# Row sums of the last two heads by ones in 32-column tiles, a 256-column part in the model's second layer, and a plan with every place moved

## The chip, the cores and the metric

The kernel runs on one core of one Trainium2 chip. The metric is device time in microseconds (us); the kernel before took 472.49 us, the median of three runs (470.97 to 474.16). Five engines share the work, each with its own queue in program order: TensorE (PE, with its weight loads shown apart as PEld), VectorE (DVE), ScalarE (ACT), GpSimd (POOL) and SyncE (SP), which here issues nearly all DMAs. Matmul results go to PSUM, from where DVE or ACT fetch them; a buffer in PSUM or SBUF can be written again only when its last reader is done.

## The reference

Two stages follow one another. The first is attention over 4 batches of 8 heads, 768 positions, 64 wide, in which a query sees only keys of its own hash bucket (six sign bits of a projection). The second is a soft mixture of experts on the attention's output.

```python
q_bits = (np.einsum('bhsd,dk->bhsk', q, proj) > 0); k_bits = (np.einsum('bhsd,dk->bhsk', k, proj) > 0)
mask = q_bucket[:, :, :, None] == k_bucket[:, :, None, :]
scores = np.where(mask, scale * np.matmul(q, k.transpose(0, 1, 3, 2)), -1e9)
attn = np.exp(scores - np.max(scores, axis=-1, keepdims=True))
out = np.matmul(attn / (np.sum(attn, axis=-1, keepdims=True) + 1e-09), v)
...
logits = x @ phi                       # x: 3072 rows of 512, phi: 512 x 32
d = softmax of logits over the rows;  slot_input = d.T @ x
h = np.maximum(slot_input[e] @ w1[e], 0.0);  slot_out[e] = h @ w2[e]     # 8 experts, 512 -> 1024 -> 512
c = softmax of logits over the slots; return c @ slot_out
```

## The kernel before

**Heads.** The 32 heads run one after another, overlapped by a plan. A head's 768 x 768 table is made six row tiles of 128 at a time. `smax` (L692) multiplies a tile's Y rows without exponent to find each row's maximum, which `most` (L701, L704) takes on DVE from one of two PSUM buffers (`p_sm`); `shift` (L730 to L733) turns a head's maxima into shifts on DVE, `shift_rows` (L740, L743) transposes them on PE, copies them on ACT and sends them into row 64 of X by a DMA. `scores` (L755) then makes the table again, in three PSUM buffers (`p_st`), and `exps` (L761) takes the exponential on ACT. `acc` (L769, L772) adds the six tiles up on POOL, for the last head's last three tiles on DVE; `av` (L782) multiplies them by v in tiles of 32 columns of the array, four at a time. A table tile is 768 columns, made as 512 and 256, so half of the `smax` and `scores` matmuls are 512 columns wide and half 256.

**Row sums.** For two heads together `pair_sum` (L794) multiplies `acc` by ones in 32-column tiles, ACT copies the result, `pair_turn` (L801, L803) transposes it on DVE and takes the reciprocal, `pair_rec` (L807, L811) transposes back. The last two heads, 30 and 31, go singly: `one_tok` (L852) loads six 128 x 128 blocks of `acc` as weights and multiplies them by one column of ones, `one_r` (L856, L857) adds eps and takes reciprocals, `one_rec` (L864) spreads them by 12 matmuls with the identity into PSUM, and `one_mul` (L869) multiplies the head's output by them. `one_log` (L879) and `one_fold` (L875) make the last batch's logits, `one_x` (L883) turns the output for the slots; then `batch_max`, `batch_exp`, `batch_turn` (L948) and `batch_slots` (L961) follow. After every batch of eight heads the same work runs in the plan as `batch_both` to `batch_arrange`. `spin_in` and `batch_spin` (L1034) turn stored weights of earlier batches.

**The plan.** No engine's order is written out line by line. Every call above gets a place, a number in slots (six slots to a head): WHEN holds the places of a typical even and odd head, FIRST those of the first heads, LAST those of the last two, counted from the end. The calls are sorted by place (L1132) and issued in that order, and each call puts its instructions, DMAs included, at the end of the queues of its engines. So a place sets the order on every engine's queue, and nothing else.

**Prologue.** `bits`, `split_hi`, `split_lo`, `first_x`, `bits_rest` prepare heads 0 and 1 on ACT, DVE and POOL; `shift_first(0)` and `rows_first(0)` (L711 to L713, L720 to L722) shift the first four row tiles of head 0, `shift_first(1)` and `rows_first(1)` the last two. `keep_busy` fills PE with idle matmuls.

**Weights.** Pieces of 512 KB of w1 and w2 are loaded by SP: 21 in the plan, one in six slots (`load_weights`), 24 more as the attention's pools are freed from slot `last - 14` on (L1134 to L1165), the rest while the model runs.

**Model.** `hidden` (L1202), `turned` (L1216), then `model` (L1255) makes four parts of 128 output columns:

```python
    PART = tuple((n // 2, n % 2 * P, P) for n in range(KC))
    for i in range(KC):
        model(i, 1)
        so = split_out(i)
        if i < KC - 1:
            begin(i + 1)
            model(i + 1, 0, range(5))
        send(so, i)
```

`split_out` (L1263, L1264) copies a part in two halves of precision, `send` (L1278, L1281) multiplies it by the slot weights in six pieces and issues the output's DMAs on SP, for the last part six of 256 KB (L1283).

Of the kernel before, what the change touches and what calls it, by code (L numbers as in the profile page):

```python
# [76 lines left out]

FIRST = {('bits', 0): -72.6747,
 ('first_x', 0): -27.9008,
 ('first_x', 1): -26.1415,  # L80
 ('first_x', 2): -26.8579,
 ('first_x', 3): -23.1972,
 ('load', 4, 0): -6.8513,
 ('load', 4, 1): -8.037,
 ('bits', 2): -24.4068,
 ('split_hi', 2): -8.1664,
 ('split_lo', 2, 0): -2.6064,
 ('split_lo', 2, 1): -1.9761,
 ('spread_y', 2): -5.503,
 ('spread_bits', 2): -10.0455,  # L90
 ('spread_l', 2): 0.6012,
 ('spread_x', 2): 9.7073,
 ('smax', 1, 0, 0): -18.3027,
 ('smax', 1, 0, 1): -7.7987,
 ('smax', 1, 1, 0): -7.7809,
 ('smax', 1, 1, 1): -16.5074,
 ('smax', 1, 2, 0): -1.6546,
 ('smax', 1, 2, 1): -7.0969,
 ('smax', 1, 3, 0): -5.3473,
 ('smax', 1, 3, 1): -10.2117,  # L100
 ('smax', 1, 4, 0): -2.2645,
 ('smax', 1, 4, 1): -10.1613,
 ('smax', 1, 5, 0): -8.0819,
 ('smax', 1, 5, 1): -8.3095,
 ('first_y', 1): -42.2836,
 ('first_y', 2): -15.549,
 ('spread_y', 1): -27.7984,
 ('spread_l', 0): -14.408,
 ('spread_bits', 1): -27.0534,
 ('bits_rest',): -34.7942,  # L110
 ('bits_copy', 0): -63.6382,
 ('bits_copy', 1): -58.3416,
 ('first_w', 0, 0): -62.1853,
 ('first_w', 0, 1): -41.4124,
 ('copy_ident',): -20.1322,
 ('bits_out',): -18.4901,
# [4 lines left out]
 ('most', 1, 0): -16.7983,
 ('most', 1, 2): -2.8602,
 ('most', 1, 3): -12.717,
 ('most', 1, 4): -0.0617,
 ('most', 1, 6): -0.8205,
 ('most', 1, 7): -8.2722,
 ('most', 1, 8): -0.5381,
 ('most', 1, 10): -4.2243,
# [1 line left out]
 ('bits_first', 1): -42.1244,  # L130
 ('split_hi', 0): -71.0276,
 ('split_lo', 0, 0): -34.7937,
 ('split_lo', 0, 1): -31.3679,
 ('spread_x', 0): -8.3415,
 ('load_v', 0): -32.8507,
 ('smax', 0, 0, 0): -43.5236,
# [1 line left out]
 ('most', 0, 0): -31.9163,
 ('exps', 0, 0): -11.5103,
 ('smax', 0, 0, 1): -39.8038,  # L140
 ('scores', 0, 0, 1): -11.555,
 ('smax', 0, 1, 0): -37.4567,
 ('scores', 0, 1, 0): -10.1798,
 ('most', 0, 2): -23.5156,
 ('exps', 0, 2): -6.5408,
 ('smax', 0, 1, 1): -63.9296,
 ('scores', 0, 1, 1): -4.3102,
 ('most', 0, 3): -32.8132,
 ('exps', 0, 3): -1.9067,
 ('smax', 0, 2, 0): -40.7538,  # L150
 ('scores', 0, 2, 0): -10.1532,
 ('most', 0, 4): -24.1099,
 ('exps', 0, 4): -6.3229,
 ('smax', 0, 2, 1): -31.6426,
 ('scores', 0, 2, 1): -5.5744,
 ('smax', 0, 3, 0): -30.4598,
 ('scores', 0, 3, 0): -2.022,
 ('most', 0, 6): -22.6441,
 ('exps', 0, 6): -0.8279,
 ('smax', 0, 3, 1): -41.857,  # L160
 ('scores', 0, 3, 1): -1.0568,
 ('most', 0, 7): -31.2096,
 ('exps', 0, 7): 0.3214,
 ('smax', 0, 4, 0): -19.3974,
 ('scores', 0, 4, 0): -13.0479,
 ('most', 0, 8): -18.0237,
 ('exps', 0, 8): -8.3163,
 ('smax', 0, 4, 1): -25.1431,
 ('scores', 0, 4, 1): -8.0065,
 ('smax', 0, 5, 0): -25.0975,  # L170
 ('scores', 0, 5, 0): -3.2765,
 ('most', 0, 10): -20.1124,
 ('exps', 0, 10): 0.0515,
 ('smax', 0, 5, 1): -29.6765,
 ('scores', 0, 5, 1): 0.6417,
 ('most', 0, 11): -20.2405,
 ('exps', 0, 11): 7.3801,
 ('av', 0, 0): -6.448,
 ('acc', 0, 1): 1.236,
 ('av', 0, 1): 0.222,  # L180
 ('acc', 0, 2): 3.5659,
 ('av', 0, 2): 2.2158,
 ('acc', 0, 3): 11.2521,
 ('av', 0, 3): 2.5799,
 ('acc', 0, 4): 12.2768,
 ('av', 0, 4): 7.1934,
 ('acc', 0, 5): 17.6795,
 ('av', 0, 5): 10.6193,
 ('spread_l', 1): -19.2874,
 ('spread_x', 1): -11.4653,  # L190
 ('load_v', 1): -62.3718,
 ('scores', 1, 0, 0): 5.8215,
 ('exps', 1, 0): 7.9587,
 ('scores', 1, 0, 1): 3.0669,
 ('scores', 1, 1, 0): 5.1281,
 ('exps', 1, 2): 7.8346,
 ('scores', 1, 1, 1): 3.5907,
 ('exps', 1, 3): 5.8224,
 ('scores', 1, 2, 0): 6.602,
 ('exps', 1, 4): 8.2456,  # L200
 ('scores', 1, 2, 1): 7.8818,
 ('scores', 1, 3, 0): 8.0524,
 ('exps', 1, 6): 8.2514,
 ('scores', 1, 3, 1): 7.1217,
 ('exps', 1, 7): 9.5937,
 ('scores', 1, 4, 0): 11.0381,
 ('exps', 1, 8): 11.4237,
 ('scores', 1, 4, 1): 9.5798,
 ('scores', 1, 5, 0): 11.0927,
 ('exps', 1, 10): 11.6836,  # L210
 ('scores', 1, 5, 1): 11.3223,
 ('exps', 1, 11): 14.6309,
 ('shift', 1): 0.3343,
 ('shift_rows', 1): 1.0244,
 ('av', 1, 0): 11.4569,
 ('acc', 1, 1): 9.0913,
 ('av', 1, 1): 12.1564,
 ('acc', 1, 2): 9.4434,
 ('av', 1, 2): 12.4636,
 ('acc', 1, 3): 16.034,  # L220
 ('av', 1, 3): 13.6761,
 ('acc', 1, 4): 18.0104,
 ('av', 1, 4): 15.8205,
 ('acc', 1, 5): 18.0227,
 ('av', 1, 5): 17.6592,
 ('load', 2, 0): -41.9391,
 ('load', 2, 1): -33.0335,
 ('load_v', 2): 15.3736,
 ('smax', 2, 0, 0): -0.969,
 ('scores', 2, 0, 0): 11.9422,  # L230
 ('most', 2, 0): 1.6034,
 ('exps', 2, 0): 12.8561,
 ('smax', 2, 0, 1): 2.6468,
 ('scores', 2, 0, 1): 19.2511,
 ('smax', 2, 1, 0): 2.7151,
 ('scores', 2, 1, 0): 20.0695,
 ('most', 2, 2): 5.8071,
 ('exps', 2, 2): 20.2977,
 ('smax', 2, 1, 1): 4.3747,
 ('scores', 2, 1, 1): 18.8979,  # L240
 ('most', 2, 3): 6.6984,
 ('exps', 2, 3): 19.3969,
 ('smax', 2, 2, 0): 5.8812,
 ('scores', 2, 2, 0): 14.0957,
 ('most', 2, 4): 9.3359,
 ('exps', 2, 4): 17.0111,
 ('smax', 2, 2, 1): 1.5133,
 ('scores', 2, 2, 1): 17.6289,
 ('smax', 2, 3, 0): 1.9085,
 ('scores', 2, 3, 0): 20.2039,  # L250
 ('most', 2, 6): 4.1541,
 ('exps', 2, 6): 20.5254,
 ('smax', 2, 3, 1): 2.3419,
 ('scores', 2, 3, 1): 18.51,
 ('most', 2, 7): 4.1671,
 ('exps', 2, 7): 18.6459,
 ('smax', 2, 4, 0): 0.3426,
 ('scores', 2, 4, 0): 20.2573,
 ('most', 2, 8): 3.8721,
 ('exps', 2, 8): 20.5597,  # L260
 ('smax', 2, 4, 1): 5.5737,
 ('scores', 2, 4, 1): 13.7623,
 ('smax', 2, 5, 0): 5.8534,
 ('scores', 2, 5, 0): 14.5864,
 ('most', 2, 10): 9.2668,
 ('exps', 2, 10): 17.0626,
 ('smax', 2, 5, 1): 2.5531,
 ('scores', 2, 5, 1): 11.9948,
 ('most', 2, 11): 5.9084,
# [1071 lines left out]
```

## Time and profile before

| | |
|---|---|
| runs | 470.97, 472.49, 474.16 us (median 472.49) |
| the profiled execution | 473.32 us, span 471.5 us |
| PE busy | 452.6 us, 96% |
| POOL, DVE, ACT busy | 342.2, 358.1, 277.2 us (73%, 76%, 59%) |
| mean granted clock of PE | 0.989 |

The span runs from the first to the last instruction; the profiled execution's own time is 1.8 us longer. A row of a timeline gives start, duration, engine, line, operation, `out<-in`, shapes and how many instructions are merged; the bracket at its end gives the idle time of that engine just before it and what ended it. Matmul rows overlap their successors, so the cost of a group of matmuls is read from start to start.

### The profile page before, as it was taken

How to read it: one execution, taken by the hardware profiler on the slowest of the kernel's cores; microseconds unless marked ns; L12 is line 12 of the kernel's file. 1: busy time of each engine (PE TensorE's matmuls, PEld its weight loads, DVE VectorE, ACT ScalarE, POOL GpSimd, SP SyncE). 2: the span in 40 equal slices, each digit the busy share in tenths (PEclk: the TensorE clock that was granted, in tenths of full speed). 3: DMA queues.
4: the chain of work that ended last, by engine and by line, in shares of the span. 5: the costliest groups of instructions: out<-in, count | busy, mean ns of one | idle time of the engine just before them, and what ended most of it. 6: DMA issues, size and time to landing. Idle time of an engine off the chain costs nothing.

```text
span 471.5 us, 11017 instructions
## 1 busy us (share of the span) xinstructions
PE 452.6 (96%) x4159; PEld 284.8 (60%) x4159; DVE 358.1 (76%) x680; ACT 277.2 (59%) x569; POOL 342.2 (73%) x209
## 2 busy tenths in 40 slices
PE   8899999999999999999999999999999999979993
PEld 6555757575756566666665566666565755553782
DVE  5766879898989897978798989898989864454241
...
GB/s 207 173 74 177 151 188 184 191 181 180 193 187 182 130 198 159 214 154 219 157 215 159 208 130 236 138 148 129 149 136 90 100 202 384 307 358 332 411 310 265
DMA packets 37704, 93.21 MB, mean 198 GB/s; under 512 B 7106, under 2 KB 13380, under 8 KB 37652
## 3 DMA queue, kind: packets, MB, share of 16 engines
...
## 4 chain that ended last, share of the span: by engine, by line
PE 78%; DVE 9%; DMA 7%; issue 2%; SPq 1%; ACT 1%; DVEq 0%; POOL 0%; ACTq 0%
PE st L755 25%; PE av L782 20%; PE smx L692 14%; DVE w L596 3%; PE qs L1255 3%; PE qh L1202 3%; DVE mx L704 3%; DMA v<-vt 2%; PE mi L794 2%; PE mi L639 2%; PE mi L819 2%; DMA w<-w 1%; SPq L600 1%; PE mi L740 1%; DMA fold<-cst 1%
## 5 line engine op out<-in xcount | busy, mean ns | idle before, releaser
L772 POOL TENSOR_TENSOR acc<-acc,pt 128x768 f32<-128x768 f32 x125 | 246.4, 1977 | 7.6 <-ACT pt L761 1.0
L761 ACT ACTIVATE pt<-st 128x512 f32<-128x512 f32 x288 | 160.3, 595 | 55.8 <-PE st L755 52.6
L755 PE MATMUL st<-XY 128*128 128x256 f32 (+1 forms) x768 | 175.0, 343 | 0.4 <-DMA XY<-mr 0.2
L704 DVE TENSOR_REDUCE mx<-smx 128x1 f32<-128x512 f32 x192 | 130.6, 688 | 20.3 <-PE smx L692 17.0
L755 PEld LDWEIGHTS st<-XY 128*128 128x128 f32 x768 | 127.3, 190 | 23.1 <-ACT pt L761 4.3
L782 PE MATMUL av<-pt,v 128*32 128x384 f32 x1536 | 136.0, 489 | 0.5 <-DMA v<-vt 0.5
L692 PE MATMUL smx<-XY 96*128 96x512 f32 (+1 forms) x384 | 116.0, 361 | 4.5 <-DVE mx L704 2.5
L692 PEld LDWEIGHTS smx<-XY 96*128 96x128 f32 x384 | 67.9, 190 | 36.4 <-DVE mx L704 15.8
L782 PEld LDWEIGHTS av<-pt,v 128*32 128x32 f32 x1536 | 46.8, 110 | 69.8 <-issue 66.4
L769 POOL TENSOR_TENSOR acc<-pt 128x768 f32<-128x768 f32 x32 | 61.1, 1908 | 32.1 <-ACT pt L761 31.9
L701 DVE TENSOR_REDUCE mx<-smx 128x2 f32<-128x512 f32 x96 | 65.7, 685 | 9.2 <-PE smx L692 8.5
L596 DVE TENSOR_TENSOR w<-raw,w 128x768 fp32r<-128x768 f32 x28 | 39.4, 1407 | 6.2 <-ACT w L592 5.6
L786 ACT COPY avs<-av 128x384 f32<-128x384 f32 x32 | 15.4, 480 | 28.3 <-PE av L782 28.3
L797 ACT ACTIVATE sm<-mi,eps 128x384 f32<-128x384 f32 x15 | 8.7, 582 | 27.1 <-PE mi L794 27.0
L592 ACT CAST w<-raw 128x768 fp32r<-128x768 f32 x30 | 23.6, 832 | 0.8 <-DMA XY<-mr 0.5
L609 ACT CAST XY<-w 64x768 fp32r<-64x768 f32 x30 | 23.4, 830 | 0.0
L811 ACT COPY r<-rt 64x12 f32<-64x12 f32 x60 | 12.0, 200 | 13.0 <-DVE rt L803 12.3
L801 DVE STREAM_TRANSPOSE sm<-sm 128x384 f32<-128x384 f32 x15 | 8.7, 577 | 13.8 <-ACT sm L797 13.8
L842 DVE TENSOR_TENSOR xq<-mi,r 128x384 f32<-128x384 f32 x30 | 16.7, 558 | 2.1
L841 DVE STREAM_TRANSPOSE mi<-avs 128x384 f32<-128x384 f32 x30 | 17.4, 579 | 1.1 <-ACT mr L743 1.1
L895 POOL TENSOR_TENSOR dl<-lacc,dl 64x384 f32<-64x384 f32 x6 | 6.0, 1008 | 16.3 <-ACT dl L893 16.1
L1255 PE MATMUL qs<-w 128*32 128x128 f32 x464 | 15.5, 274 | 0.0
...
## 6 DMA issues: line engine op xcount, KB each, us to landing
...
```

The source lines that it names most:

```text
L592: nc.scalar.copy(st[h]["w4"][:, 2 * x], st[h]["raw", x])
L596: (nc.vector if h > 2 else nc.gpsimd).tensor_tensor(out=w[:, 2 * x + 1], in0=st[h]["raw", x], in1=w[:, 2 * x], op=ALU.subtract)
L609: nc.scalar.copy(s["Y"][0:64, x], s["w4"][0:64, 2 * x])
L692: nc.tensor.matmul(pt[:, o:o + b - a], s["Y"][0:96, 0, t * P:(t + 1) * P], s["Y"][0:96, 1, a:b], start=True, stop=True)
L701: nc.vector.tensor_reduce(out=mx[:, n - 1:n + 1], in_=s["sm_ps", n - 1].rearrange("p (a x) -> p a x", a=2), axis=AX.X, op=ALU.max)
L704: nc.vector.reduce_max(out=mx[:, n:n + 1], in_=s["sm_ps", n], axis=AX.X)
L755: nc.tensor.matmul(pt[:, o:o + b - a], x[:, 1, i * P:(i + 1) * P], x[:, 0, a:b], start=first, stop=not first)
L761: nc.scalar.activation(s["P", n // 4][:, 512 * u:512 * u + 512], s["st_ps", n - (n % 4 == 2)], AF.Exp, scale=D ** -0.5)
L769: nc.gpsimd.tensor_tensor(out=s["acc"], in0=pr[:, 0:S], in1=pr[:, S:2 * S], op=ALU.add)
L772: eng.tensor_tensor(out=s["acc"], in0=s["acc"], in1=pr[:, a * S:(a + 1) * S], op=ALU.add)
L782: nc.tensor.matmul(s["av"][2 * e + 32 * c:2 * e + 32 * c + 32, 0:HC], s["v"][:, i, e:e + 32], pr[:, o + c * HC:o + (c + 1) * HC], start=(i ...
L1255: nc.tensor.matmul(pos[i][32 * j:32 * j + 32, 0:w], hTs[g][:, f, 32 * j:32 * j + 32], wt[1, x, 2 * g + f // 4, j][:, (f % 4) * HM + o:(f % ...
```

## The change

- The last two heads' sums are made by `one_sum` (four products of ones in 32-column tiles, as in `pair_sum`), `one_r` transposes them on DVE from PSUM, adds eps and takes the reciprocal, and `one_rec` transposes back on DVE; 18 matmuls of each head go. The transposed rows lie in `sm` for head 30 and in `dl` for head 31.
- The model's parts are 256, 128 and 128 columns instead of four of 128. The first part is split at once and sent as two: one send between the fifth and sixth block of the next part's first layer group, the other after it.
- The last of the six closing output DMAs is issued by ScalarE.
- All numbers in WHEN, FIRST and LAST are new. The keys are the same but for `one_sum` in the place of `one_tok`.

```diff
 WHEN = {...
- 'smax': [[-5.5404, -5.239, -5.1892, -3.4795, -4.556, -5.0483, -4.843, -3.5583, -2.8991, -3.0436, -2.9566, -3.1005], [-7.8798, -7.8794, -7.7178, -7.0216, -6.4263, -3.51, -3.3611, -6.2386, -3.9477, -1.0552, -0.461, -1.6316]],
- 'shift': [-2.121, 0.7267],
- 'av': [[9.338, 9.6759, 9.8253, 9.848, 9.9231, 9.9801], [6.073, 6.1257, 6.303, 6.4394, 6.7221, 7.1612]],
- 'pair_sum': 21.1732,
- 'pair_turn': 21.4204,
- 'pair_rec': 21.5496,
- 'pair_log': 21.2289,
- 'pair_x': [22.4828, 26.9143],
- 'pair_add': 21.7661,
- 'load_weights': 4.0141,
+ 'smax': [[-5.732, -5.5796, -5.0917, -3.7223, -4.1498, -3.8513, -3.8386, -4.1503, -2.8752, -2.6442, -2.5991, -3.4423], [-7.7507, -7.4218, -7.3813, -7.0158, -5.1741, -3.5779, -3.5007, -5.8225, -3.877, -1.248, -1.1291, -2.1688]],
+ 'shift': [-2.0119, -0.0964],
+ 'av': [[7.9858, 8.0552, 9.4992, 9.6029, 9.6963, 9.9894], [7.0927, 7.2218, 7.5071, 7.7352, 7.8092, 7.8291]],
+ 'pair_sum': 21.407,
+ 'pair_turn': 21.6968,
+ 'pair_rec': 21.9832,
+ 'pair_log': 21.875,
+ 'pair_x': [25.5532, 32.2093],
+ 'pair_add': 23.3238,
+ 'load_weights': 45.5566,
...
 FIRST = {...
- ('shift_first', 0): -18.7053,
- ('rows_first', 0): -16.6615,
- ('rows_first', 1): -13.9076,
- ('scores', 0, 0, 0): -12.1508,
- ('most', 1, 11): -1.8467,
+ ('shift_first', 0): -24.3878,
+ ('rows_first', 0): -22.3433,
+ ('rows_first', 1): -18.2833,
+ ('scores', 0, 0, 0): -18.6378,
+ ('most', 1, 11): -14.8751,
...
 LAST = {...
- ('batch_spin', -3, 1): -2.7637,
- ('av', -1, 0): -3.8828,
- ('one_mul', -2): 1.7622,
+ ('batch_spin', -3, 1): 13.6867,
+ ('av', -1, 0): -1.7406,
+ ('one_mul', -2): 5.1149,
...
-    def one_tok(h, pool):
-        s = st[h]
-        pt = s["tok"] = pool.tile([P, 512], F32, name=names[pool])[:, 0:6].rearrange("p (k c) -> p k c", k=3)
-        for k in range(3):
-            for c in range(2):
-                o = c * HC + k * P
-                nc.tensor.matmul(pt[:, k, c:c + 1], s["acc"][:, o:o + P], ones[:, 0:1], start=True, stop=True)
+    def one_sum(h, pool):
+        pt = pool.tile([P, 512], F32, name=names[pool])
+        for n in range(4):
+            c = n % 2
+            nc.tensor.matmul(pt[32 * n:32 * n + 32, 0:HC], ones, st[h]["acc"][:, c * HC:(c + 1) * HC],
+                             start=True, stop=True)
+        st[h]["sum"] = pt[:, 0:HC]
 
     def one_r(h):
-        r = st[h]["r"] = dp.tile([P, 3, 2], F32, name="r1", bufs=1)
-        nc.vector.tensor_scalar_add(r, st[h]["tok"], EPS)
+        tt = st[h]["rs"] = dp.tile([P, HC], F32, name="dl" if h == BH - 1 else "sm", bufs=1)
+        nc.vector.transpose(tt, st[h]["sum"])
+        r = st[h]["r"] = dp.tile([P, NT * 2], F32, name="rt", bufs=1)
+        nc.vector.tensor_scalar_add(r, tt.rearrange("p (j x) -> p j x", x=32)[:, :, 0], EPS)
         nc.vector.reciprocal(out=r, in_=r)
 
-    def one_rec(h, pool):
-
-        pt = pool.tile([P, 512], F32, name=names[pool])
-        for k in range(3):
-            for n in range(4):
-                nc.tensor.matmul(pt[32 * n:32 * n + 32, k * P:(k + 1) * P],
-                                 st[h]["r"][:, k, n % 2:n % 2 + 1].broadcast_to([P, 32]), ident, start=True, stop=True)
-        st[h]["rs"] = pt[:, 0:HC]
+    def one_rec(h):
+        nc.vector.transpose(st[h]["rs"], st[h]["r"][:, :, None].broadcast_to([P, NT * 2, 32]))
...
-    PART = tuple((n // 2, n % 2 * P, P) for n in range(KC))
+    PART = (0, 0, 2 * P), (1, 0, P), (1, P, P)
...
-                nc.sync.dma_start(out=out[i, u // 2, :, cols], in_=ob[:, cols])
+                (nc.scalar if u == 5 else nc.sync).dma_start(out=out[i, u // 2, :, cols], in_=ob[:, cols])
...
-    for i in range(KC):
+    n = len(PART)
+    done = 0
+    for i in range(n):
         model(i, 1)
         so = split_out(i)
-        if i < KC - 1:
+        parts = [(so[:, o:o + P], done + o // P) for o in range(0, PART[i][2], P)]
+        done += len(parts)
+        if i < n - 1:
             begin(i + 1)
             model(i + 1, 0, range(5))
-        send(so, i)
-        if i < KC - 1:
+        send(*parts[0])
+        if i < n - 1:
             model(i + 1, 0, range(5, FC))
+        for part in parts[1:]:
+            send(*part)
```

## Rows read from the trace of the kernel before

**Rows 1.** The page: engine totals, and a costly group (busy, mean ns, idle before).

```profile
PE 452.6 (96%) x4159; PEld 284.8 (60%) x4159; DVE 358.1 (76%) x680; ACT 277.2 (59%) x569; POOL 342.2 (73%) x209
...
L704 DVE TENSOR_REDUCE mx<-smx 128x1 f32<-128x512 f32 x192 | 130.6, 688 | 20.3 <-PE smx L692 17.0
```

**Rows 2.** Busy time by stretch: length, PE, PEld, DVE, ACT, POOL, clock, DMA share, GB/s.

```profile
22.00:24.00 2.00, 0.71 (x3) 0.48 (x3) 1.41 (x3) 2.00 (x5) 2.00 (x2) 1.00 0.86 327
24.00:26.00 2.00, 2.00 (x11) 0.73 (x11) 0.33 (x1) 0.52 (x1) 1.09 (x1) 0.57 0.44 98
...
200.00:220.00 20.00, 19.96 (x172) 11.75 (x171) 16.45 (x31) 12.48 (x26) 16.13 (x9) 1.00 0.75 195
418.00:420.00 2.00, 0.14 (x8) 0.14 (x16) 1.10 (x5) 1.48 (x5) 0.00 (x0) 1.00 1.03 397
420.00:422.00 2.00, 2.00 (x48) 1.03 (x40) 0.67 (x5) 0.91 (x3) 0.00 (x0) 0.55 0.58 207
```

**Rows 3.** PE's timeline in a pair of heads in mid-run: start, duration, group.

```profile
182.61 3.41 PE L782 MATMUL av<-pt,v 128*32 128x384 f32 x40
185.95 0.30 PE L740 MATMUL mi<-ident,mz 128*72 128x128 f32 x1
...
187.50 0.39 PE L692 MATMUL smx<-XY 96*128 96x512 f32 x1
187.73 0.63 PE L755 MATMUL st<-XY 128*128 128x512 f32 x2
...
188.90 0.40 PE L692 MATMUL smx<-XY 96*128 96x512 f32 x1
189.23 4.08 PE L782 MATMUL av<-pt,v 128*32 128x384 f32 x48
193.24 0.74 PE L692 MATMUL smx<-XY 96*128 96x512 f32 x3
```

**Rows 4.** PE's timeline late in the attention, one tile of `av` by itself.

```profile
395.72 0.85 PE L782 MATMUL av<-pt,v 128*32 128x384 f32 x8 [0.52 <-DMA v<-vt]
```

**Rows 5.** Waits from 60 to 350 us: waiter, releaser, total us, times, longest.

```profile
PEld smx L692 <- DVE mx L704: 11.0, 26, 1.0
...
PEld smx L692 <- DVE mi L841: 6.2, 10, 0.6
```

**Rows 6.** DVE's timeline in the same pair, between the row sums and the shift.

```profile
183.50 0.56 DVE L830 TENSOR_TENSOR mi<-mi,sm 128x384 f32<-128x384 f32 x1
...
184.96 0.17 DVE L733 SCALAR_TENSOR_TENSOR mz<-mi,mz 128x6 f32<-128x6 f32 x1
```

**Rows 7.** Timelines of PE and ACT in the prologue.

```profile
13.32 1.68 ACT L621 CAST XY<-w 32x768 fp32r<-32x768 f32 x2
...
18.38 1.71 PE L755 MATMUL st<-XY 128*128 128x512 f32 x6
...
23.79 0.39 PE L692 MATMUL smx<-XY 96*128 96x256 f32 x1 [0.78 <-DVE mx L701]
```

**Rows 8.** Timelines of PE, POOL and DVE around the last two heads' end.

```profile
404.73 1.39 PE L852 MATMUL mi<-ones,acc 128*128 128x1 f32 x12
...
405.60 1.83 POOL L772 TENSOR_TENSOR acc<-acc,pt 128x768 f32<-128x768 f32 x1
...
408.56 3.09 DVE L772 TENSOR_TENSOR acc<-acc,pt 128x768 f32<-128x768 f32 x3 [0.96 <-ACT pt L761]
...
415.39 0.56 DVE L869 TENSOR_TENSOR avs<-avs,smx 128x384 f32<-128x384 f32 x1
```

**Rows 9.** Groups by line: count, busy us, mean ns, idle before.

```profile
L807 DVE STREAM_TRANSPOSE sm<-rt 128x384 f32<-128x384 f32 x15 | 8.7, 578 | 0.5
```

**Rows 10.** PE's and SP's timelines in the model.

```profile
434.79 5.36 PE L1202 MATMUL qh<-w,siT 128*32 128x512 f32 x48
...
453.49 3.91 PE L1255 MATMUL qs<-w 128*32 128x128 f32 x128
...
463.63 4.06 SPq L1283 DMA_DIRECT2D out<-w  x6
```

More of the change, by code (lines that the diff above doesn't have):

```diff
@@ L78 @@
[L78 to L116, printed above, removed]
- ('shift_first', 0): -18.7053,
- ('rows_first', 0): -16.6615,
- ('shift_first', 1): -16.3608,
- ('rows_first', 1): -13.9076,
[L121 to L128, printed above, removed]
- ('most', 1, 11): -1.8467,
[L130 to L136, printed above, removed]
- ('scores', 0, 0, 0): -12.1508,
[L138 to L269, printed above, removed]
- ('exps', 2, 11): 16.833,
- ('shift', 2): 9.4458,
- ('shift_rows', 2): 9.9626,
- ('spread_y', 3): 4.3291,
- ('spread_bits', 3): 4.9954,
- ('spread_l', 3): 0.9099,
- ('spread_x', 3): 4.5792}
@@ new lines @@
+WHEN = {'load': -18.5189,
+ 'bits': -14.5612,
+ 'bits_over': -14.0399,
+ 'split_hi': -11.818,
+ 'split_lo': [-9.7194, -8.485],
+ 'spread': [[-10.6854, -10.5862, -5.0657, -3.8156], [-9.18, -8.7643, -9.3302, -8.5267]],
+ 'load_v': [1.0924, 1.154],
+ 'smax': [[-5.732, -5.5796, -5.0917, -3.7223, -4.1498, -3.8513, -3.8386, -4.1503, -2.8752, -2.6442, -2.5991, -3.4423], [-7.7507, -7.4218, -7.3813, -7.0158, -5.1741, -3.5779, -3.5007, -5.8225, -3.877, -1.248, -1.1291, -2.1688]],
+ 'scores': [[3.8691, 7.2977, 7.2977, 3.6037, 2.2454, 6.9487, 7.2847, 5.6465, 8.1314, 7.5049, 7.5088, 5.457], [2.3655, 3.2704, 3.2792, 2.1621, 5.1218, 2.4254, 2.4774, 2.9368, 4.9013, 5.1691, 6.2997, 4.4125]],
+ 'shift': [-2.0119, -0.0964],
+ 'shift_rows': [-2.0037, 1.283],
+ 'acc': [[8.5607, 10.3766, 11.591, 12.6422, 13.213], [4.6481, 8.0689, 9.5473, 9.5584, 10.2149]],
+ 'av': [[7.9858, 8.0552, 9.4992, 9.6029, 9.6963, 9.9894], [7.0927, 7.2218, 7.5071, 7.7352, 7.8092, 7.8291]],
[5 more added lines that the diff above has]
+ 'pair_add': 23.3238,
+ 'batch_both': 25.5169,
+ 'batch_max': 31.1051,
+ 'batch_exp': 31.7595,
+ 'batch_turn': 32.6557,
+ 'batch_scale': 54.1951,
+ 'batch_slots': 33.2203,
+ 'batch_weigh': 32.9896,
+ 'batch_share': 33.5438,
+ 'batch_arrange': 33.6389,
+ 'load_weights': 45.5566,
+ 'most': [[-5.1628, -4.9644, -3.3582, -4.0032, -3.6843, -3.9715, -2.3197, -2.4373, -2.8774], [-6.1815, -5.7422, -4.8687, -3.5042, -2.2071, -3.5047, -2.3707, -0.206, -0.4661]],
+ 'exps': [[6.8105, 7.328, 5.4338, 2.8674, 8.4247, 6.8427, 8.7299, 8.3013, 6.811], [2.8264, 3.6517, 2.7976, 6.0494, 3.3607, 3.7533, 5.4883, 6.6009, 5.324]]}
@@ L1113, in lsh_attention_soft_moe @@
     h = BH - 1
-    for g, pool, pool2 in ((h - 1, p_mi, p_mi), (h, p_st, p_sm)):
-        at(last, one_tok, g, pool)
+    for g, pool in ((h - 1, p_mi), (h, p_st)):
+        at(last, one_sum, g, pool)
         at(last, one_r, g)
-        at(last, one_rec, g, pool2)
+        at(last, one_rec, g)
         at(last, one_mul, g)
```

445 lines of the change are left out of this document (309 added, 136 removed).

## The prediction

> **What bounds the kernel now.** First the engine totals: TensorE is busy for 452.6 of 471.5 us, DVE for 358.1, POOL for 342.2 [rows 1]. Then busy time by stretch, because a share of the whole span hides stages. In mid-run PE has 19.96 of 20 us and DVE 16.45, so there a change pays only through what PE does, or through waits that hide behind a busy PE. Two other stretches stand out: PE nearly stops and then runs at half clock, at 22 to 24 us (0.71 of 2.00, then clock 0.57) and at 418 to 420 us (0.14, then 0.55) [rows 2]. Last, PE's timeline and the waits, for the price of another order [rows 3 to 5]. The profiled execution took 473.32 us, 0.83 above the median of the runs (472.49); the sum is made against 473.3.
>
> **Places in mid-run: the loss.** A place only sets the order in the queues. What it can cost on PE is a change between 32-column calls (`av`, pair sums, their turns) and full-width ones (`smax`, `scores`). One `av` adds (4.08 - 0.85) / 5 = 0.646 us to a run of its kind [rows 3, 4]. Five of them take 185.95 - 182.61 = 3.34 from start to start, 0.11 over 5 x 0.646; six take 193.24 - 189.23 = 4.01, 0.13 over: the price of leaving. Entering shows in an `smax` of 512 columns: 0.33 to the next start before `av` (188.90 to 189.23), 0.23 before `scores` (187.50 to 187.73): 0.10 [rows 3]. A run of 32-column calls so costs about 0.23. With both lists of places sorted between slots 24 and 180, I count 57 changes between the two kinds before and 84 after: 13.5 more runs, **+3.1**.
>
> A page states the same mechanism: the Trainium skill, "TensorEngine Tiling (Array Packing)", section "Tiling Modes", says under its key properties that changing the tiling mode drains TensorE. The trace agrees, with 0.10 to 0.13 at a change, and by that rule alone mid-run would be slower.
>
> **Places in mid-run: the gain.** From 60 to 350 us PE's weight loads for `smax` wait 11.0 us for maxima and 6.2 for the transposes of `pair_x` on DVE, 17.2 together [rows 5]. In the odd head three of nine `most` leave the crowd about the row sums: from 0.58, 0.68 and 0.62 to -2.21, -0.21 and -0.47, while `smax` moves by under 1.3 slots in all twelve calls. `pair_x` moves 3 and 5 slots back, and with it its DVE transposes, its product and PE's turns behind it; `pair_add` (two operations, the first 0.56 [rows 6]) now lies behind the even head's shift instead of ahead; the batch work that follows moves by some 0.3 to 7 slots, on all engines. Nothing of this adds an instruction. Three of nine maxima go, so I take a third of the waits, **-5.7**; no row says which ones. Net **-2.6**; bounds -5.5 (half the waits) and +3.1 (none). The weight pieces begin 41.5 slots later on SP, among the same loads of heads, at a DMA share of 0.75 [rows 2]: nothing here; if that cover went, a head's load would be late and `scores` next. In the tail they count, below.
>
> **Prologue.** `shift_first(0)` is taken after six maxima instead of eight, so two maxima of 0.69 (mean 688 ns [rows 1]) fall behind it, and `scores(0,0,0)` goes ahead of `rows_first(1)`. Scores start at 18.38; ACT's casts of X end at 13.32 + 1.68 = 15.00 and the row copies come after them, so at most 3.4 is there [rows 7]; I take the two maxima, -1.4. At 23.79 `smax` of head 1 waits 0.78 on a maximum [rows 7]: `most(1, 11)` stood behind `most(1, 2)` and is now ahead of it, as its `smax` is. That stall is worth 2.00 - 0.71 = 1.3, the half clock after it 0.9 (0.43 of 2 us) [rows 2]. ACT is full there too (2.00 of 2), so I take a quarter, -0.6. Together **-2.0**; bounds -3.6 (all of it) and +1.4 (two maxima late instead).
>
> **Tail, to the last exponentials.** From before the last scores go: `one_tok(30)`, 1.39 for a product of the size of an `av` tile, 0.65: -0.7 [rows 8]; one `batch_spin`, four small matmuls, at a third of the 1.39 for twelve: -0.5; one `av` tile, -0.65. That is -1.8 for PE. But POOL's last sum ends at 405.60 + 1.83 = 407.43 and DVE's sums start at 408.56, so at most 1.1 shows [rows 8]. Against it, `av` waits 0.52 for the load of v [rows 4], and by the new places one more piece of 512 KB lies ahead of that load on SP, 1.3 us at 397 GB/s [rows 2], of which I count 0.5. **-0.6**; bounds -1.1 and +1.3.
>
> **Tail, the row sums.** From DVE's last sum (408.56 + 3.09 = 411.65) to the end of `one_mul` (415.39 + 0.56) lie 4.30 us [rows 8]. After the change all of it queues on DVE, head 30's `one_r` too, which lies behind the last sum (0.78 against -0.02): for each head a transpose of 0.58, two small operations of 0.17, a transpose of 0.58 and a product of 0.56, 2 x 2.06 = 4.1 [rows 6, 8, 9]. The matmuls of `one_rec` and `one_tok(31)` go, in PE's idle time. A transpose out of PSUM has no row; I take that out of SBUF as the nearest. **-0.2**; bounds -0.8 (the handoffs to PE gone as well) and +0.8 (both such transposes at twice the time).
>
> **Tail, the clock.** The spin now stands among the calls after `one_log`, in the stretch where PE has 0.14 of 2 us before it runs the slots at 0.55 [rows 2]. If it and the turns keep PE at work, 0.9 in two microseconds is there: **-0.6**; bounds -1.2 and +0.3 (the slots queue behind it).
>
> **Model.** For a group of four 32-column matmuls 128 columns cost 3.91 / 32 = 0.122 us and 512 columns 5.36 / 12 = 0.447 [rows 10]. By the line between them 256 cost 0.23, for 2 x 0.122: 32 groups, -0.5; by columns alone (0.447 / 2) -0.65. **-0.6**; bounds -0.8 and +0.5. The copy of twice the width is covered by five of the eight next blocks, 10 groups or 1.2 us; if that fell short, `send` would be late. The last part stays at 128.
>
> **Last output.** SP issues its six DMAs over 4.06 us [rows 10]. With one moved to ACT's queue a sixth of that, 0.7, is the most; but ACT has that block to copy first. **0**; bounds -0.7 and +0.4.
>
> Sum: -2.6 - 2.0 - 0.6 - 0.2 - 0.6 - 0.6 = -6.6, from 473.3: **466.7**.
>
> **The rivals.** (1) Half the waits go, and all of the prologue's 3.6: 466.7 - 2.9 - 1.6 = **462.2**. For it: the waits have few kinds. Against: part of a weight load's wait lies beside a running matmul. (2) The changes of width are paid and no wait goes, the new places not doing on DVE what they say: 466.7 + 5.7 = **472.4**. For it: PE at 19.96 of 20. The drain rule of the page above is this rival. (3) Slower: the even head's `shift_rows`, one full-width call on PE, blocks all behind it when `shift` is late. Now it has 185.95 - (184.96 + 0.17) = 0.82 us in hand [rows 3, 6]; `pair_add` behind it gives 2 x 0.56, two `av` fewer ahead take 1.29: 0.65 is left. One late maximum (0.69) uses it, two overdraw it by 0.73, in 13 pairs 9.5 us: 472.4 + 9.5 = **481.9**, and 478.7 with two pairs in three. It decides from the second late maximum on. Against: the maxima come earlier by their places.
>
> **How the numbers follow.** Chances: the forecast 0.45, (1) 0.15, (2) 0.25, (3) 0.15. The forecast by itself spans 463.5 (mid-run at its bound) to 470.5 (a third less of each gain and v late); the range takes in (1) and (2) with their smaller bounds, **461.0 to 476.0**, and leaves out (3) and a little below. Over 1% is 4.7 us, about what a measurement tells from no change: below 467.8 or above 477.2. Faster: 0.34 of the forecast and (1); same: the other 0.11, 0.24 of (2), 0.02 of (3); slower: 0.13 of (3) and 0.01 of (2). So 0.49, 0.37, 0.14.
>
> **What would show it.** Right: first scores near 17, no half clock at 24, waits of `smax` on DVE down by a third, some 14 more runs of 32-column calls at 0.23 each, the last exponentials a microsecond earlier, 0.23 for a group of 256 columns. Wrong: waits as before (2); idle PE ahead of `shift_rows` in pair after pair (3); a late load of a head or of v; POOL's last sum, not PE, setting DVE's start; the last output landing later.

## The result

The changed kernel takes 469.24 us (median of 18 runs, 464.91 to 474.05) against 472.77 in the runs of the kernel before beside it; the ratio is 0.9907 [0.9881, 0.9933] (in brackets the 95% interval), 4.4 us. The ratio leaves out four slow runs of the changed kernel (472.12 to 474.05, each over 1.5% above its fastest); with all 18 runs of each kernel the medians differ by 3.5. The forecast was 466.7 against 473.3, or 6.6. The profiled execution has a span of 467.4 against 471.5: 4.1 less. The experiments' ratios are each against the kernel before, run on the same chip.

The engine totals after:

```profile
PE 450.5 (96%) x3975; PEld 275.4 (59%) x3975; DVE 359.3 (77%) x683; ACT 279.5 (60%) x568; POOL 337.7 (72%) x209
```

Where the 4.1 us lie is read from marks that both traces have: ACT's copy of a head's output (L786), DVE's last sum, the slots, the first group of the model, the last send. The marks of before that no row above shows:

```profile
41.89 0.48 ACT L786 COPY avs<-av 128x384 f32<-128x384 f32 x1 [0.98 <-PE av L782]
88.72 0.48 ACT L786 COPY avs<-av 128x384 f32<-128x384 f32 x1 [1.69 <-PE av L782]
363.73 0.48 ACT L786 COPY avs<-av 128x384 f32<-128x384 f32 x1 [0.36 <-PE av L782]
...
419.86 2.56 PE L961 MATMUL st<-xq,avs 64*32 64x256 f32 x48 [2.18 <-DVE avs L948]
439.96 1.06 PE L1255 MATMUL qs<-w 128*32 128x128 f32 x32
462.38 0.73 PE L1278 MATMUL qh<-ct,w 128*128 128x512 f32 x3 [0.76 <-DVE w L1264]
```

The same marks after, heads 0, 4 and 27, then DVE's last sums, the slots and the model:

```profile
38.17 0.48 ACT L786 COPY avs<-av 128x384 f32<-128x384 f32 x1 [1.55 <-PE av L782]
85.83 0.48 ACT L786 COPY avs<-av 128x384 f32<-128x384 f32 x1 [1.51 <-PE av L782]
359.75 0.48 ACT L786 COPY avs<-av 128x384 f32<-128x384 f32 x1 [0.83 <-PE av L782]
...
404.08 3.01 DVE L772 TENSOR_TENSOR acc<-acc,pt 128x768 f32<-128x768 f32 x3
...
415.40 1.99 PE L957 MATMUL st<-xq,avs 64*32 64x256 f32 x48 [1.38 <-DVE avs L944]
436.77 1.91 PE L1251 MATMUL qs<-w 128*32 128x256 f32 x32
458.60 0.73 PE L1274 MATMUL qh<-ct,w 128*128 128x512 f32 x3 [0.77 <-DVE w L1260]
```

| stretch | before | after | difference | forecast |
|---|---|---|---|---|
| start to head 4 | 88.72 | 85.83 | -2.9 | -2.0 |
| head 4 to head 27 | 275.01 | 273.92 | -1.1 | -2.6 |
| to the end of DVE's last sum [rows 8] | 47.92 | 47.34 | -0.6 | -0.6 |
| to the slots | 8.21 | 8.31 | +0.1 | -0.2 |
| slots to the model's first group | 20.10 | 21.37 | +1.3 | -0.6 |
| to the last send | 22.42 | 21.83 | -0.6 | -0.6 |
| to the end | 9.1 | 8.8 | -0.3 | 0 |

Busy time by stretch after. The first two answer to the stall of [rows 2], the next three to the stretch around the slots, the last to mid-run from head 4 to head 27:

```profile
22.00:24.00 2.00, 1.92 (x11) 1.41 (x11) 1.99 (x4) 1.89 (x3) 0.19 (x1) 1.00 0.19 58
24.00:26.00 2.00, 2.00 (x14) 1.42 (x16) 1.53 (x4) 2.00 (x4) 2.00 (x2) 1.00 0.58 198
...
414.00:416.00 2.00, 0.62 (x25) 0.49 (x32) 1.12 (x5) 1.60 (x5) 0.00 (x0) 1.00 1.03 393
416.00:418.00 2.00, 2.00 (x43) 1.09 (x23) 0.92 (x4) 0.40 (x1) 0.00 (x0) 0.58 0.60 186
418.00:420.00 2.00, 2.00 (x11) 2.00 (x11) 0.32 (x2) 0.86 (x2) 0.00 (x0) 0.50 1.04 401
...
85.83:359.75 273.92, 272.70 (x2344) 168.97 (x2344) 242.90 (x449) 186.32 (x377) 229.99 (x139) 1.00 0.66 173
```

The stall and the half clock of the prologue are gone. The half clock behind the slots is there still, and longer: some 7 us (416 to 423) where it was under 4 (from 420). In mid-run PE is busy 0.34 us longer than before and idle 1.43 less; the row of before is

```profile
88.72:363.73 275.01, 272.36 (x2344) 171.01 (x2344) 241.82 (x447) 184.77 (x378) 233.60 (x138) 1.00 0.65 170
```

The waits of [rows 5] after, in the same 60 to 350 us; a wait of `smax` on `pair_x` (L841) is listed no more:

```profile
PEld smx L692 <- DVE mx L704: 8.6, 17, 0.6
```

It looks as if half of the 17.2 us were left, but these sums mix two kinds of wait. The weight loads show it one by one, first in a pair before (with the transpose that is named as a releaser), then in a pair after:

```profile
192.25 0.58 DVE L841 STREAM_TRANSPOSE mi<-avs 128x384 f32<-128x384 f32 x1
193.24 0.53 PEld L692 LDWEIGHTS smx<-XY 96*128 96x128 f32 x3 [0.62 <-DVE mi L841]
194.94 0.19 PEld L692 LDWEIGHTS smx<-XY 96*128 96x128 f32 x1 [0.47 <-DVE mx L704]
...
92.98 0.19 PEld L692 LDWEIGHTS smx<-XY 96*128 96x128 f32 x1 [0.62 <-DVE mx L704]
94.58 0.19 PEld L692 LDWEIGHTS smx<-XY 96*128 96x128 f32 x1 [0.35 <-DVE mx L704]
100.57 0.30 PEld L755 LDWEIGHTS st<-XY 128*128 128x128 f32 x2 [0.62 <-issue]
```

The transpose ended at 192.83, 0.41 before the load that it is said to have released. The same 0.62 us stands ahead of the first wider weight load behind a run of 32-column calls, be it of `smax`, `scores` or `shift_rows`, and whichever releaser is named: in 22 of 28 such places before and 38 of 41 after, by PEld's timeline from 60 to 350 us. So it is the end of the run and not a wait on DVE. What is left as waits for maxima are those behind another full-width load: 24 before, 9.7 us, and 7 after, 2.4 us. Of the 17.2 us 7.4 were ends of runs (ten put down to `pair_x`, two to maxima), of the 8.6 us 6.2.

And the third run of 32-column calls that an ordinary pair now has, on PE: `smax` before it takes 0.56 for two calls (98.58 to 99.14) where two inside take 0.47, and the two `av` take 1.43 up to the next `scores`, 0.14 more than twice 0.646. Counted in the timeline from 66 to 360 us before and 63 to 356 after, there are 28 and 40 runs of 32-column calls in all.

```profile
98.58 0.63 PE L692 MATMUL smx<-XY 96*128 96x512 f32 x2
99.14 1.50 PE L782 MATMUL av<-pt,v 128*32 128x384 f32 x16
100.57 0.73 PE L755 MATMUL st<-XY 128*128 128x512 f32 x2
```

### The profile page after: what moved, and what is told of

The parts are those of the page before. It is cut to its first block, busy times and chain, and to the rows that moved or that the text cites. A ratio compares the mean times of both kernels' runs of the same rounds, so it can differ in the third digit from the quotient of the medians.

```text
span 467.4 us, 10616 instructions
## 1 busy us (share of the span) xinstructions
PE 450.5 (96%) x3975; PEld 275.4 (59%) x3975; DVE 359.3 (77%) x683; ACT 279.5 (60%) x568; POOL 337.7 (72%) x209
## 4 chain that ended last, share of the span: by engine, by line
PE 90%; DMA 4%; DVE 3%; ACT 1%; issue 1%; SPq 0%; DVEq 0%; ACTq 0%
PE st L755 29%; PE av L782 26%; PE smx L692 15%; PE qh L1198 3%; PE qs L1251 3%; PE mi L639 3%; PE mi L794 3%; PE mi L819 2%; DMA w<-w 1%; PE mi L740 1%; PE mi L957 1%; DMA fold<-cst 1%; DVE mx L704 1%; PE qh L1274 1%; PE av L548 1%
## 5 line engine op out<-in xcount | busy, mean ns | idle before, releaser
L772 POOL TENSOR_TENSOR acc<-acc,pt 128x768 f32<-128x768 f32 x125 | 243.7, 1954 | 8.2 <-ACT pt L761 1.4
L761 ACT ACTIVATE pt<-st 128x512 f32<-128x512 f32 x288 | 163.4, 596 | 56.5 <-PE st L755 44.9
L755 PE MATMUL st<-XY 128*128 128x512 f32 (+1 forms) x768 | 177.1, 345 | 2.8 <-ACT pt L761 2.2
L755 PEld LDWEIGHTS st<-XY 128*128 128x128 f32 x768 | 123.6, 189 | 32.0 <-issue 12.5
L782 PE MATMUL av<-pt,v 128*32 128x384 f32 x1536 | 137.7, 489 | 0.0
L692 PEld LDWEIGHTS smx<-XY 96*128 96x128 f32 x384 | 69.7, 190 | 27.7 <-DVE mx L704 11.0
L769 POOL TENSOR_TENSOR acc<-pt 128x768 f32<-128x768 f32 x32 | 58.7, 1834 | 37.5 <-ACT pt L761 37.5
L786 ACT COPY avs<-av 128x384 f32<-128x384 f32 x32 | 15.4, 481 | 42.2 <-PE av L782 42.2
L797 ACT ACTIVATE sm<-mi,eps 128x384 f32<-128x384 f32 x15 | 8.7, 582 | 23.8 <-PE mi L794 20.4
L841 DVE STREAM_TRANSPOSE mi<-avs 128x384 f32<-128x384 f32 x30 | 17.5, 583 | 0.1
L1198 PE MATMUL qh<-w,siT 128*32 128x512 f32 x128 | 15.4, 636 | 0.0
L1251 PE MATMUL qs<-w 128*32 128x128 f32 (+1 forms) x360 | 14.9, 304 | 0.0
L639 PE MATMUL mi<-raw,pb 128*32 128x384 f32 x120 | 13.9, 507 | 0.4 <-DMA raw<-qk 0.4
```

What stands on the lines that cost most here:

```text
L639: nc.tensor.matmul(pts_b[j // 2 if h == 0 else 0][32 * j:32 * j + 32, 0:HC], pb[:, 32 * (j // 2):32 * (j // 2) + 32], st[h]["raw", j // 2] ...
L692: nc.tensor.matmul(pt[:, o:o + b - a], s["Y"][0:96, 0, t * P:(t + 1) * P], s["Y"][0:96, 1, a:b], start=True, stop=True)
L755: nc.tensor.matmul(pt[:, o:o + b - a], x[:, 1, i * P:(i + 1) * P], x[:, 0, a:b], start=first, stop=not first)
L761: nc.scalar.activation(s["P", n // 4][:, 512 * u:512 * u + 512], s["st_ps", n - (n % 4 == 2)], AF.Exp, scale=D ** -0.5)
L769: nc.gpsimd.tensor_tensor(out=s["acc"], in0=pr[:, 0:S], in1=pr[:, S:2 * S], op=ALU.add)
L772: eng.tensor_tensor(out=s["acc"], in0=s["acc"], in1=pr[:, a * S:(a + 1) * S], op=ALU.add)
```

## The experiments

**The three lists of places, one at a time.** `WHEN`, `FIRST` or `LAST` of before in the changed kernel:

```diff
-WHEN = {'load': -18.5189, ...
+WHEN = {'load': -17.7191, ...        # the whole list of before
```

Expected of e1 (when old):

> The changed kernel with the old WHEN (the places of the typical pairs); all else is new. Theory from the two traces: the new places take away the idle time of PE at the ends of the batches (5.65 us in 28 runs of 32-column calls before, 1.81 in 40 runs after, 60 to 360 us) and pay 12 runs at 0.23 = 2.8 us for it; so an ordinary pair goes back from 23.72 to 23.61 us, three pairs with a batch's end from 72.9 to 73.7, and the total rises by about 1.0. The forecast's theory (a third of the 17.2 us of DVE waits gone): the total rises by 2.6. The rival that the changes of width are paid for nothing: the total falls by 3.

0.9964 [0.9930, 0.9997]. An ordinary pair went back to 23.62 us exactly:

```profile
86.77:110.39 23.62, 23.58 (x196) 14.94 (x195) 20.39 (x37) 15.53 (x31) 19.66 (x10) 1.00 0.70 188
```

From head 4 to 27 it took 274.94 us, 1.0 more than the changed kernel, as the theory has it and not as the forecast had it. The total rose by more, some 2.7 us by the ratios (0.9964 against 0.9907), because the lists do not part cleanly: from head 0 to head 4 it lost 1.6 (49.29 against 47.66), and 2.1 from head 27 to DVE's last sum, where the new LAST joins (49.40 against 47.34).

Expected of e2 (first old):

> The changed kernel with the old FIRST (places of the first heads). Theory from the traces: the stall of PE at 22 to 24 us comes back, with half clock for some four microseconds behind it; first scores stay near 18.4 (18.38 before, 18.50 after); head 3's output is copied 3.0 us later than in the changed kernel (72.4 against 69.4), total +3. The forecast's theory: +1.4 from first scores that come later, +0.6 from the stall, total +2.0.

Here head 2's first two `av` come ahead of the exponentials that fill their tiles. 1.0020 [0.9982, 1.0058], some 5 us over the changed kernel where 3 was expected. The stall is back, but the clock stayed at full behind it:

```profile
22.00:24.00 2.00, 0.79 (x5) 0.37 (x3) 1.32 (x3) 2.00 (x5) 2.00 (x2) 1.00 0.73 267
24.00:26.00 2.00, 1.88 (x14) 1.09 (x15) 0.79 (x3) 0.84 (x2) 1.43 (x1) 1.00 0.45 100
...
89.94 0.48 ACT L786 COPY avs<-av 128x384 f32<-128x384 f32 x1 [1.51 <-PE av L782]
```

Head 4 is 4.1 later than in the changed kernel and 1.2 later than before. In this order the stall costs without any half clock, and from head 0 to head 4 the old first heads take longer with the new pairs than with the old (49.25 against 46.83); how much of either the early `av` of head 2 make is not shown.

Expected of e3 (last old):

> The changed kernel with the old LAST, but the new places of the calls that sum the last two heads and of the pair before them (with the old ones DVE would wait for itself). Theory from the traces: the three last sums on DVE start about 0.6 later against head 27; PE's half clock behind the slots lasts about 4 us as before instead of 7, which gives back 1.3; total -0.7. The forecast's theory: both terms of the tail are lost, total +1.2.

1.0034 [1.0001, 1.0067]. It tells nothing of the tail's terms, and LAST was not tried in another way: with these places head 31 is summed ahead of its last two `acc`, DVE's three last sums are pulled apart (408.15 to 413.26), and the chain that was to be compared is another one.

**The model's parts.**

```diff
-    PART = (0, 0, 2 * P), (1, 0, P), (1, P, P)
+    PART = tuple((n // 2, n % 2 * P, P) for n in range(KC))
```

Expected of e4 (part128):

> The changed kernel with four parts of 128 columns in the model's second layer. Theory from the traces and the forecast alike: from the start of the first model group to the last send 22.4 us instead of 21.8, total +0.6. Rival: the gain between the two traces came from a weight that landed earlier, total 0.

0.9893 [0.9840, 0.9945], which does not differ from the changed kernel. The stretch does: from the model's first group to the last send 23.40 us (435.15 to 458.55) against 21.83 in the changed kernel and 22.42 in the one before. It is 1.6 and not 0.6, because PE also stood for 0.9 where it did not in either (to the end of the span 1.0 is left: 31.65 against 30.63):

```profile
435.15 1.06 PE L1251 MATMUL qs<-w 128*32 128x128 f32 x32
442.23 0.27 PE L1251 MATMUL qs<-w 128*32 128x128 f32 x1 [0.54 <-issue]
447.87 0.52 PE L1251 MATMUL qs<-w 128*32 128x128 f32 x9 [0.36 <-issue]
```

In this profiled execution the clock held behind the slots, so the model began 1.6 earlier than in the changed kernel. The profile names no releaser, and the DMA share does not tell: it is 1.01 from 440 to 444 us, and 1.03 in the changed kernel, which does not stand there. So the 0.6 of PE's own time stands, the rest is open, and the total of this run can't show either.

**What a run of 32-column calls costs.** First the same two `av` moved, in either kernel:

```diff
- 'av': [[7.9858, 8.0552, 9.4992, ...       # changed kernel
+ 'av': [[9.41, 9.45, 9.4992, ...
- 'av': [[9.338, 9.6759, 9.8253, ...        # kernel before
+ 'av': [[7.9858, 8.0552, 9.8253, ...
```

Expected of e5 (av late):

> The changed kernel with the even head's first two av at 9.41 and 9.45 instead of 7.99 and 8.06, so that they lie in the run of 32-column calls that follows. Theory (a run costs 0.23 us): an ordinary pair takes 23.49 instead of 23.72, total -2.5 to -3. Rival: the early av free the tiles of pt for exps, which then come late; the pair gets longer, 23.9 or more, total +2.

1.0187 [1.0122, 1.0252]; a pair took 24.85 and not 23.49. The theory of a plain price fell, and the rival that I had named does not explain it either: in that pair the loads of `scores` wait only 0.2 for exponentials. PE now waits on DVE's maxima, which stand back to back:

```profile
96.72 0.50 PE L692 MATMUL smx<-XY 96*128 96x512 f32 x1 [0.42 <-DVE mx L704]
...
102.12 0.51 PE L692 MATMUL smx<-XY 96*128 96x256 f32 x2 [0.31 <-DVE mx L704]
```

In one pair `smax` and its weight loads wait 3.2 us for maxima, against 1.0 in the changed kernel; without the 0.62 that ends a run of `av` in both, it is 2.6 against 0.35. The two `av` are 1.3 us of work for PE while DVE catches up. They cost a change of width and are themselves what shortens the waits.

Expected of e6 (before av split):

> The kernel before with the even head's first two av at 7.99 and 8.06, as the changed kernel has them, and nothing else: one more run of 32-column calls per pair. Theory (a run costs 0.23): an ordinary pair takes 23.84 instead of 23.61, total +2.8. Rival: weight loads and matmuls hide the change of width, total 0, or earlier free pt tiles make it faster.

Here too head 2's first two `av` come ahead of their exponentials. 1.0508 [1.0459, 1.0557], 24 us: far beyond both. In the old pair these places lie ahead of the exponentials on ACT, so PE waits in them; one `av` takes 1.30 instead of 0.65, and they make two runs instead of one. By the rows below they cost some 1.0 more than within a run (1.30 and 0.78 from start to start for twice 0.65, and two entries). The first ordinary pair grew by 1.7 (25.30 against 23.62); the rest was not traced:

```profile
104.11 1.37 PE L782 MATMUL av<-pt,v 128*32 128x384 f32 x8
105.41 0.51 PE L755 MATMUL st<-XY 128*128 128x256 f32 x2
105.84 0.85 PE L782 MATMUL av<-pt,v 128*32 128x384 f32 x8
```

Neither run measures the price alone. The next one does; it cuts a run in two and moves nothing:

```diff
+        if h % 2 and 4 < h < 28 and i == 2:
+            nc.tensor.matmul(s["av"][:, 0:4], ident, zeros, start=False, stop=False)
```

Expected of e11 (split run):

> The changed kernel with one full-width matmul of 4 columns (it adds zeros to four columns of the output) behind the third of the six av of odd heads 5 to 27: the run of 32-column calls is cut in two, and nothing else moves. Theory: leaving and entering cost 0.23 and the small matmul 0.05 to 0.1, so an ordinary pair takes 24.0 instead of 23.72, total +3 to +3.9. Rival: the change of width costs nothing by itself (0.1 is what the small matmul takes): 23.8, total +1.

0.9989 [0.9967, 1.0010], 3.9 us over the changed kernel; a pair took 24.00, both as expected.

```profile
88.57 2.14 PE L784 MATMUL av<-pt,v 128*32 128x384 f32 x24
90.64 0.39 PE L787 MATMUL av<-zeros,ident 128*128 128x4 f32 x2
90.96 2.14 PE L784 MATMUL av<-pt,v 128*32 128x384 f32 x24
93.03 0.50 PE L694 MATMUL smx<-XY 96*128 96x512 f32 x1
```

From 88.57 to 93.03 the six `av` take 4.46, against 4.00 uncut in the changed kernel (88.98 to 92.98): 0.46 for one change there and back and a matmul of 4 columns with its full-width weights. The pair grew by 0.28 only, and its one wait for a maximum, 0.35, went to nothing. The change of width is paid, and in a pair whose PE waits for DVE a part of it comes back.

**The stall in the prologue.** Head 1's `smax` and `most` alone:

```diff
- ('most', 1, 11): -1.8467,
+ ('most', 1, 11): -14.8751,       # and the other 20 keys ('smax', 1, ...), ('most', 1, ...)
```

Expected of e7 (before max1):

> The kernel before with head 1's smax and most at the new places of FIRST, and nothing else: the maxima are then taken in the order in which smax fills the two buffers. Theory: the stall at 22 to 24 us goes and with it the half clock at 24 to 28, total -2.5 to -3. Rival: the stall is ACT's, which is full there, and stays; total 0 to -0.6.

1.0044 [1.0015, 1.0073], 2.1 us slower: neither the theory nor the rival. PE no longer waits for those maxima, but it stands still earlier (busy 1.14 of the 2 us from 18 to 20, then half clock at 22 us) and again at 24 us, with ACT full:

```profile
22.00:24.00 2.00, 2.00 (x9) 1.90 (x9) 0.94 (x2) 1.58 (x3) 0.00 (x0) 0.50 0.87 349
24.00:26.00 2.00, 1.45 (x7) 1.02 (x7) 1.48 (x3) 2.00 (x5) 1.64 (x1) 0.92 0.00 0
```

My reading of the wait at 23.79 [rows 7] falls. The whole of FIRST takes the stall away:

Expected of e9 (before first new):

> The kernel before with the new FIRST (places of the first heads) and nothing else. Theory: the new order of the first heads as a whole takes away the stall at 22 to 24 us and the half clock that can follow; head 3's output at 70.5 instead of 72.4 as in the run with the old WHEN, total -2 to -3, whatever the clock. Rival: FIRST and WHEN only gain together (the pair at the joint of the two lists waits); total 0 to -1.

0.9974 [0.9947, 1.0002], 1.2 us, not clear of none. PE is busy 1.93 of the 2 us from 22 to 24, and head 0 is out at 38.02 instead of 41.89, but head 4 at 87.29, 1.4 earlier and not 2.9. With the old WHEN 2.4 us of the 3.9 go again between heads 0 and 4; with the new one 0.8 (47.66 against 46.83). By the profiles the two lists are worth more together.

**The clock behind the slots.** Idle matmuls of `ident` where PE stands:

```diff
+    def warm(n):
+        pt = p_mi.tile([P, 512], F32, name="mi")
+        for _ in range(n):
+            nc.tensor.matmul(pt[:, 0:P], ident, ident, start=True, stop=True)
...
+    at(last + .1, warm, 3)
+    at(last + 12, warm, 3)
+    at(last + 60, warm, 4)      # kernel before: only this one, with 7
```

Expected of e8 (warm):

> The changed kernel with ten idle matmuls of ident on PE in the tail: three ahead of the sum of head 31, three ahead of its logits, four ahead of the last slots, where PE stood for 1.0, 1.1 and 1.4 us. Theory: the granted clock stays at full behind the slots instead of half from 416 to 423 us, the first hidden group takes 8.8 instead of 10.0 us and the slots 1.5 instead of 1.9: total -1.5 to -3. Rival: the idle matmuls delay what is behind them and the clock falls all the same: total +0.5.

0.9881 [0.9847, 0.9915]. PE is busy 1.57 instead of 0.62 of the 2 us ahead of the slots, and the clock stays up:

```profile
414.76:416.76 2.00, 1.57 (x14) 1.34 (x13) 1.13 (x5) 1.74 (x7) 0.00 (x0) 1.00 1.02 391
416.76:418.76 2.00, 2.00 (x53) 1.38 (x53) 1.21 (x8) 0.66 (x2) 0.00 (x0) 1.00 0.65 234
```

From the slots to the model 18.73 us instead of 21.37, and the slots come no later (8.30 behind the last sum).

Expected of e12 (warm again):

> The changed kernel with ten idle matmuls in the tail, as before, timed in more rounds. Theory: it holds the clock in every run, so its times spread less than those of the changed kernel and its ratio to the kernel before is 0.987 to 0.989, against 0.9907 for the changed kernel. Rival: the changed kernel holds its clock in most runs anyway; ratio 0.990 to 0.991.

The kernel of e8 again: 0.9898 [0.9872, 0.9925], median 467.08 (465.80 to 469.30), again 18.73 us there. It beats the kernel before; that it beats the changed kernel is not shown, since the intervals lie over each other. The rival is not ruled out: without idle matmuls the clock also stayed up behind the slots in the profiles of e1, e4, e5 and e11 (18.73 each) and fell in the changed kernel's own and that of e2 (20.01).

Expected of e10 (before warm):

> The kernel before with seven idle matmuls of ident on PE ahead of the last slots, where PE stood for 2.2 us, and nothing else. Theory: the clock stays at full behind the slots; from the slots' start to the first group of the model 18.7 us instead of 20.1 (18.73 in the runs of the changed kernel with full clock, 20.10 before); total -1.4 to -2. Rival: other stretches of idle PE ahead, or the model itself, bring the clock down; total 0.

0.9998 [0.9975, 1.0022], no gain. From the slots to the model it took 18.74 instead of 20.10, as expected. But the seven matmuls ran partly at the lower clock themselves and put the slots off by 0.9 (9.09 behind the last sum instead of 8.21), and the model then stood twice for something that the profile does not name:

```profile
417.00:420.00 3.00, 3.00 (x20) 2.60 (x19) 1.52 (x7) 0.88 (x4) 0.00 (x0) 0.73 1.03 404
420.00:422.00 2.00, 2.00 (x54) 1.19 (x52) 1.23 (x7) 1.50 (x4) 0.00 (x0) 1.00 0.33 135
...
449.27 0.31 PE L1261 MATMUL qs<-w 128*32 128x128 f32 x3 [0.30 <-issue]
455.30 2.60 PE L1261 MATMUL qs<-w 128*32 128x128 f32 x85 [0.64 <-issue]
```

## Why the prediction was nearly right

The direction, the range and the size within a third hold: 4.4 of 6.6 us (3.5 by the medians of all runs). By my own split, though, 469.24 counts as the same (0.37) and not as faster (0.49), which began below 467.8. The terms hold less well: by the table mid-run gave 1.5 less than forecast and the clock 1.9 less, the prologue 0.9 more.

- **Mid-run, the loss** (+3.1): right. I counted 13.5 more runs and took 0.23; the traces have 12 more, entering and leaving show as 0.09 and 0.14 in the rows after, and cutting a run cost 0.46 with a small matmul in between. The rule of the Trainium skill, "TensorEngine Tiling (Array Packing)", section "Tiling Modes", that a change of mode drains TensorE, agrees with that run; it gives no price.
- **Mid-run, the gain** (-5.7): the step that failed, by its size and twice over. Of the 17.2 us that I took for waits on DVE only 9.7 were such waits; the rest were ends of runs of 32-column calls, which come with the changes of width and do not go. Of the 9.7, 7.3 went, three quarters and not a third. And they were worth about half of their length: in the cut run a wait of 0.35 bought 0.18 (0.46 - 0.28), which would make 3.8 of the 7.3, an estimate; in the two traces 12 x 0.23 = 2.8 were paid and 1.1 won, so 3.9 came back. I had priced a microsecond of a weight load's wait as one of time, though the first rival said that part of it lies beside a running matmul. That 5.7 is not further off is luck: too few waits at too high a price.
- **Mid-run, the net** (-2.6): -1.1 in the two traces, and less sure than it looks. The first two ordinary pairs, heads 4 to 8, are 0.10 longer with the new WHEN (23.70 to 23.72 against 23.57 to 23.67, but for one of 23.92). What is won lies at the ends of the batches, and that varies: from head 8 to head 14, over one batch's end, 72.5 to 74.3 with the new places, 73.7 in all with the old. Over all profiles with unmoved and uncut `av`, head 4 to 27 takes 274.9 to 275.2 with the old WHEN (five) and 273.9 to 275.4 with the new (six); the means, 275.0 and 274.5, are 0.5 apart. With the new places four later ordinary pairs take 24.0 to 24.9 (one of 24.0 with the old), in one of them with PE idle 0.81 for the rows of `shift_rows`, in another 1.01 for an exponential.
- **Two terms were one.** I summed the loss and the gain as if they were independent. The late `av` of e5 show that the run which costs 0.23 is the work that keeps PE off the waits: without it the waits for maxima behind full-width loads are 17.8 us and not 2.4, from 60 to 350 us.
- **Prologue** (-2.0): right in size, wrong in its parts. The first scores came at 18.50, not near 17, although DVE took the shift's maxima 0.9 earlier (14.16 against 15.05): `rows_first(0)` stands behind other products in PE's queue. The gain came with the end of the stall and of the half clock behind it, which lasted 4 us (0.57, then 0.58 from 26 to 28) and not the 2 that I had counted; I had taken a quarter of both, and through head 1's maxima, which e7 refutes. How it parts between stall and clock is open, since e2, with the stall alone, was 2.5 late at head 0; so is which calls of FIRST take the stall away. The term itself is clear of the scatter: ACT's copy for head 4 stands at 85.3 to 85.9 in all six profiles with both new lists and unmoved early `av`, at 88.7 and 89.3 in the two with both old.
- **Tail to the last sum** (-0.6): -0.6 in the two profiles. But e7, e9 and e10, with the old tail, took 47.2 over this stretch, and e2, e4, e5, e8, e11 and e12, with the new one, 46.8 to 47.6: the gain is not shown beyond the pair of profiles.
- **Row sums** (-0.2): +0.1, in every profile that left this chain as it was (8.29 to 8.31 against 8.21 to 8.22). The chain on DVE takes 4.41 from the last sum to the end of `one_mul`, where I had 4.1. The transposes out of PSUM cost no more than the others (0.57 and 0.58); the reciprocal took 0.23 and not 0.17, and the rest is steps between instructions:

```profile
407.01 0.57 DVE L856 STREAM_TRANSPOSE sm<-mi 128x384 f32<-128x384 f32 x1
...
407.83 0.23 DVE L859 RECIPROCAL rt<-rt 128x12 f32<-128x12 f32 x1
...
410.94 0.56 DVE L865 TENSOR_TENSOR avs<-avs,dl 128x384 f32<-128x384 f32 x1
```

- **Clock** (-0.6): +1.3 in the profiled execution, -1.4 (18.73) in e1, e4, e5 and e11, which have the new tail and no idle matmuls. Without idle matmuls the clock fell behind the slots in all four profiles with the old tail (20.0 to 21.4 from the slots to the model, mean 20.4, PE idle in the 2 us ahead) and in two of six with the new (mean 19.4, PE busy 0.62 or 0.63); so the reason of the forecast, work for PE in that stretch, is borne out, but not in every execution. It differs from run to run, as the mean granted clock does: 0.982 to 0.996 over the runs of the kernel before, 0.985 to 0.998 over those of the changed one but for one (0.946). Taking a part of the gain was fair; the one profile would have told the wrong sign.
- **Model** (-0.6): -0.6, and in most profiles more. The line between two widths gave the 256-column group: 436.77 to 438.61 for eight groups is 0.23 each. But from the model's first group to the last send all eight profiles with the new parts take 21.83 or 21.84, and the six with four parts of 128 take 22.42 to 23.96: in four of these PE stands for 0.8 to 0.9 in all, with no releaser named (e4 and e10 above, e6 and e7 too). Why, is open.
- **Last output** (0): from the last send to the end 8.8 instead of 9.1, but other profiles have 8.3 to 9.1 with either queue; not settled.

Rival (3), `shift_rows` late in every pair, did not come: PE has no idle time ahead of it in the pairs after.
